# Sums for layer 2's logits placed in the other arms of layer 1's weight splits

## The chip, the cores and the metric

The kernel runs on one core of a Trainium2 chip. The metric is the time of the whole program on the device, in microseconds. A core has the engines TensorE (PE in the profile; its weight loads are PEld), VectorE (DVE), ScalarE (ACT), GpSimd (POOL) and SyncE (SP, which issues most of the DMAs). Each works through its own list of instructions in order, and they meet at semaphores.

## What is computed

An attention over pooled keys feeds two layers of a mixture of experts over 4608 tokens of 512 values, with 8 experts and 1024 hidden units. The change lies in the first of these layers, and in the gating of the second that is computed beside it.

```python
def _moe_ref(x, modality_id, w_gate, modality_bias, w1, w2):
    logits = x @ w_gate + modality_bias[modality_id]
    e_idx = np.argmax(logits, axis=1)
    ...                                   # gate_w: softmax of the logits, at e_idx
    for e in range(E):
        mask = e_idx == e
        h = np.maximum(x[mask] @ w1[e], 0.0)
        out[mask] = gate_w[mask, None] * (h @ w2[e])

def _moe2_ref(x, w_skip, w_gate, w1, w2):
    skip_score = x @ w_skip               # x: what layer 1 gives
    do_compute = skip_score > 0
    logits = x[do_compute] @ w_gate       # 8 logits a token
    ...                                   # as above; out = x + y where do_compute
```

So layer 2 needs nine dot products of 512 values for each token that layer 1 has finished: eight logits and the skip score. The kernel makes them on DVE.

## The kernel before

Layer 1 takes the tokens sorted by expert, in blocks of 256 (`T`). `Layer.body1(i, end)` writes out block `i`; what follows speaks of blocks 6 to 17. All engine work is in the order in which the code issues it; no scheduler moves it.

**The two products.** The first product is eight calls `m.gemm1(i, f)` (12 matmuls each, L1413): a hidden slice `f` of 128 for the 256 tokens. Numbers are split into a high and a low part, so three matmuls stand for one: `xh,w1h`, `xl,w1h`, `xh,w1l`. Behind every odd `f` ACT makes `hh` (the rectified high part) and DVE `hl` (the low part, L1418) for two slices at once. The second product is `m.gemm2(i, t, ...)` for each half `t` of the block's tokens (24 matmuls each, L1462: `w2h,hh`, `w2l,hh`, `w2h,hl` for `f` = 0 to 7). In the midst of `gemm2(i, 0)` PE transposes the next block's tokens (`next_x`, after `f` = 2 and 4), from which ACT makes `xh` and DVE `xl` (L1366). A block that is only half full skips `gemm2(i, 1)`. Block 13 of this input is one.

**A new expert.** Weights are split too. When block `i+1` has another expert than block `i` (the register `anew` tells it), the arms of four `If`s are taken: two of `split_w1_if` in block `i` (slices 0 to 3 ahead of `gemm2(i, 0)`, 4 to 7 behind it) and two of `split_w2_if` in block `i+1` (behind its `f` = 1 and `f` = 3). Each arm holds four casts on ACT (`w1h` or `w2h`) and four subtractions on DVE (`w1l`, L1333, or `w2l`, L1354). Among blocks 7 to 16 only 9 and 14 bring a new expert, and their arms run in full; the others skip them.

**The sums.** When half `t` of block `i` is done, `posts` puts nine sums on a list, `m.todo`: `logit`, one DVE instruction over 512 values (`hr`, L1743) with a short read of its accumulator (`lg`). So there are 18 a block. Behind the second half's nine stand the block's `picks`: `first` (ten small POOL operations, L1674 to L1684, and a maximum on DVE, `rt_mx`) and `second` (a maximum on DVE, `rt_my`, which waits for POOL's last `rt_eq`, then seven POOL operations, L1691 to L1696, that end in `M` and `rti`, then the block's store and scatter). `m.drip(n)` issues the next `n` entries. The calls of `drip` in `body1` are the order by hand: (1,1,1,2,1,2,1,1) behind the eight slices of the first product, one behind four or five of the slices in `gemm2(i, 0)`, and seven behind the second `split_w1_if`. The sums and picks of block `i` are thus worked off under block `i+1`.

**The ranks.** Behind `f` = 4 of the first product `rank` is called for the block before the last: two small matmuls on PE (`R`, L1722 and L1723) that read `M` and `rti`, then five short DVE operations (L1727 to L1731) and POOL work. PE stands until `rti` is there.

Of the kernel before, what the change touches and what calls it, by code (L numbers as in the profile page):

```python
# [1179 lines left out]
class Moe:  # L1180
# [154 lines left out]
    def load_split(self, i):  # L1335
        ET = mybir.EngineType
        self.anew = self.nc.values_load(self.g.r1.split[0:1, i:i + 1], min_val=0, max_val=1,
                                        engines=[ET.Activation, ET.DVE])

    def split_w1_if(self, fs):  # L1340

        with self.tc.If(self.anew > 0):  # L1342
            for f in fs:
                self.split_w1(f)
# [412 lines left out]
    def settle(self, i):  # L1757
        while any(x[0] <= i for x in self.todo):
            self.drip()

    def drip(self, n=1):
        while n > 0 and self.todo:
            _, cost, f = self.todo.pop(0)
            f()
            n -= cost


class Layer:
# [28 lines left out]
    def second(self):  # L1797

        m, g = self.m, self.m.g
        bg = g.bg  # L1800
        for f in range(8):
            m.gemm1(1, f)
            bg.tick()
            bg.tick()
        m.gemm2(1, 0, self.epilogue)
        bg.flush()
        self.gather(2)
        self.gather(3)
        self.load_regs(2)
        self.load_w1(2)  # L1810
        self.load_w2(2)
        m.load_split(2)
        m.split_w1_if(range(8))
        m.drip(7)
        m.gemm2(1, 1, self.epilogue, {3: lambda: m.xT(2, 0, m.ps_t("ps_x")),
                                      5: lambda: m.xT(2, 1, m.ps_t("ps_x")),
                                      6: lambda: m.gates1(2, m.sp)})
        m.gates2(2, m.sp)
        m.drip(5)
# [39 lines left out]
    def body(self, i):  # L1859
# [40 lines left out]
        with cmp.Else():  # L1900
            self.finish(i, full, turn, False)

    def body1(self, i, end):

        m = self.m
        late = i == self.n_static - 1
        ranks = m.ranks
        m.ranks = []
        for f in range(8):
            m.gemm1(i, f)  # L1910
            if f in (1, 3):
                m.split_w2_if(range(2 * f - 2, 2 * f + 2))
            m.drip(((0, 0, 1, 1, 1, 1, 2, 2) if late else (1, 1, 1, 2, 1, 2, 1, 1))[f])
            m.g.bg.tick()
            if f in (4, 6) and ranks:
                m.rank(ranks.pop(0))
            if f == 5 and i == self.n_static - 2:
                m.places2()
            if f == 6 and late:
                m.gather2(i + 1)  # L1920
                m.load_w1_parts(2, m.e2, end, range(4))
        m.rank_all(ranks)
        m.g.bg.flush()
        m.g.bg.pace = 2
        full = self.load_full(i)
        more = i + 1 < NBLK or end is not None
        if i + 1 < NBLK:
            self.load_w2(i + 1)
        if end is not None:
            m.load_w2_parts(2, m.e2, end)  # L1930

        def next_x(t):
            if t == 0 and end is not None:
                m.gates1(i + 1, m.sp)
            m.xT(i + 1, t, m.ps_t("ps_x"))
            if t == 1:
                m.gates2(i + 1, m.sp)

        if more:
            m.load_split(i + 1)  # L1940
            if end is None:
                m.gates1(i + 1, m.sp)
            m.split_w1_if(range(4))
        if end is None:
            at = {f: m.drip for f in ((0, 1, 5, 6) if i > 8 else (0, 1, 3, 5, 6))}
        elif late:
            at = {f: m.drip for f in (0, 1, 3, 5)}
        else:
            n = sum(x[1] for x in m.todo) - 2
            at = {f: partial(m.drip, (n + j) // 5) for j, f in enumerate((0, 1, 3, 5, 6))}  # L1950
            at[7] = m.drip
        if more and not late:
            at.update({2: lambda: next_x(0), 4: lambda: next_x(1)})
        m.gemm2(i, 0, self.epilogue, at)
        if late:
            _, _, second = m.todo.pop(0)
            m.drip(3)
            next_x(0)
            next_x(1)
            second()  # L1960
        if more:
            m.split_w1_if(range(4, 8))
        if end is None:
            m.drip(7)
        elif not late:
            m.drip()
        with m.tc.If(full > 0):
            m.gemm2(i, 1, self.epilogue)
# [126 lines left out]
```

## Time and profile before

| | us |
|---|---|
| runs (three) | 941.18, 945.1, 945.74 |
| median | 945.1 |
| profiled execution | 943.7 |
| its span, first to last instruction | 941.9 |
| PE busy | 893.1 (95% of the span) |
| DVE busy | 704.7 (75%) |
| POOL busy | 511.9 (54%) |
| ACT busy | 367.8 (39%) |
| mean granted TensorE clock | 0.981 |

In the profile a row names a line of the code, an engine, an operation, the tile written and the tiles read. In brackets stands how long the engine had been idle and what ended that. The clock is that of TensorE, granted by the throttle, as a share of full speed: 1.00 is 2.4 GHz, and its lower level, 1.2 GHz, would be 0.50. Block 7's first product starts at 367.87 us, block 9's at 415.05, block 10's at 444.33, block 13's at 515.09, block 14's at 533.67 and block 15's at 566.61.

### The profile page before, as it was taken

The numbers are of one execution on the slowest core, as the hardware profiler recorded it, in microseconds if no ns is written. First come the engines' busy times: TensorE is split into PE (matmuls) and PEld (weight loads), VectorE is DVE, ScalarE is ACT, GpSimd is POOL, SyncE is SP. The second block draws the span as 40 slices with busy tenths as digits, with TensorE's granted clock in tenths as the row PEclk, the third lists the DMA queues.
The fourth block names the chain that finished last, engine by engine and source line by source line (L and its number), as shares of the span: only waits on it lengthen the run. The fifth ranks groups of instructions, "written<-read, shape, count | busy, mean of one in ns | idle before, by whom it ended". The sixth has DMA issues, their size and how long they took to land. (4 is left out here: it accounts for less than half of the span.)

```text
span 941.9 us, 19066 instructions
## 1 busy us (share of the span) xinstructions
PE 893.1 (95%) x6231; PEld 803.2 (85%) x6231; DVE 704.7 (75%) x1816; ACT 367.8 (39%) x727; POOL 511.9 (54%) x762
## 2 busy tenths in 40 slices
PE   7899989899999999998999989999999999999995
PEld 6799889888899999987999869999888988979993
DVE  5467886787777888889877898777665777688663
ACT  3466656453222222251222422213413556565551
POOL 5766797303246647666766556575653443445442
PEclk9999999999999999999999999999989999999998
DMA  9999965513212211441224521227115673671341
GB/s 233 216 255 264 256 195 157 193 62 121 69 58 86 74 38 64 143 153 66 83 83 130 172 79 64 75 72 253 58 65 156 206 230 126 202 244 36 111 161 44
DMA packets 86141, 126.07 MB, mean 134 GB/s; under 512 B 13192, under 2 KB 50104, under 8 KB 85866
## 3 DMA queue, kind: packets, MB, share of 16 engines
q1 hardware_dynamic: 75386, 96.68, 33.4%
q0 software_dynamic: 10608, 27.67, 9.7%
q8 instruction: 63, 1.03, 0.5%
q14 instruction: 84, 0.69, 0.2%
HBM read 182.09 MB, written 39.50 MB: 235 GB/s over the span
## 5 line engine op out<-in xcount | busy, mean ns | idle before, releaser
L1413 PE MATMUL ps_g<-xh,w1h 128*128 128x256 f32 x896 | 256.4, 286 | 2.5 <-DVE o L1652 1.5
L1413 PE MATMUL ps_g<-xl,w1h 128*128 128x256 f32 x896 | 253.3, 283 | 2.2 <-DVE xl L1366 2.2
L1413 PE MATMUL ps_g<-xh,w1l 128*128 128x256 f32 x896 | 252.7, 282 | 0.0
L1743 DVE CUSTOM_DVE_ANT_0 hr<-x,W 128x512 bf16<-128x512 f32 x324 | 228.1, 704 | 19.1 <-DVEq L1342 6.3
L1462 PE MATMUL ps_g<-w2h,hh 128*128 128x512 f32 x464 | 190.6, 411 | 3.0 <-ACT w2h L1353 1.6
L1462 PE MATMUL ps_g<-w2h,hl 128*128 128x512 f32 x464 | 185.4, 400 | 6.2 <-DVE hl L1418 6.1
L1462 PE MATMUL ps_g<-w2l,hh 128*128 128x512 f32 x464 | 184.6, 398 | 0.0
L1413 PEld LDWEIGHTS ps_g<-xh,w1h 128*128 128x128 f32 x896 | 169.7, 189 | 7.2 <-issue 2.3
L1413 PEld LDWEIGHTS ps_g<-xl,w1h 128*128 128x128 f32 x896 | 169.2, 189 | 4.0 <-DVE xl L1366 3.0
L1413 PEld LDWEIGHTS ps_g<-xh,w1l 128*128 128x128 f32 x896 | 169.5, 189 | 0.0
L1417 ACT ACTIVATE hh<-ps_g 128x512 fp32r<-128x512 f32 (+1 forms) x116 | 67.7, 584 | 248.8 <-PE ps_g L1413 246.6
L1418 DVE SCALAR_TENSOR_TENSOR hl<-ps_g,hh 128x512 fp32r<-128x512 f32 (+1 forms) x116 | 77.5, 668 | 64.1 <-ACT hh L1417 40.0
L911 POOL TENSOR_SCALAR OB<-iota,BB,pay 128x128 bf16<-128x128 bf16 x126 | 111.7, 894 | 21.5 <-DVE BB L899 21.4
L1462 PEld LDWEIGHTS ps_g<-w2h,hl 128*128 128x128 f32 x464 | 88.2, 190 | 29.5 <-DVE hl L1418 7.7
L1462 PEld LDWEIGHTS ps_g<-w2h,hh 128*128 128x128 f32 x464 | 88.6, 191 | 21.4 <-issue 2.5
L1462 PEld LDWEIGHTS ps_g<-w2l,hh 128*128 128x128 f32 x464 | 88.5, 191 | 16.7
L1354 DVE TENSOR_TENSOR w2l<-w2r,w2h 128x512 fp32r<-128x512 f32 x112 | 75.3, 710 | 6.6 <-ACT w2h L1353 4.6
L1333 POOL TENSOR_TENSOR w1l<-w1r,w1h 128x512 fp32r<-128x512 f32 x35 | 45.3, 1314 | 59.7 <-ACT w1h L1330 59.4
L1709 POOL DMA_INDIRECT out_dram<-x,dsi x38 | 47.6, 1252 | 44.5 <-DMA out_dram<-x,dsi 16.8
L1353 ACT CAST w2h<-w2r 128x512 fp32r<-128x512 f32 x112 | 63.9, 617 | 0.0
L1330 ACT CAST w1h<-w1r 128x512 fp32r<-128x512 f32 x112 | 63.7, 620 | 0.5 <-ACT hh L1417 0.5
L1323 POOL DMA_INDIRECT xg<-xd,gidx x38 | 44.1, 1162 | 33.7 <-DVE rs_lo L1174 16.5
(298 smaller groups left out, 1399.9 us busy)
## 6 DMA issues: line engine op xcount, KB each, us to landing
w1r<-in_moe_w_dram SPq DMA_DIRECT2D x128, 512.0 KB
w2r<-in_moe_w_dram SPq DMA_DIRECT2D x124, 512.0 KB
x2s<-x SPq DMA_DIRECT2D x19, 522.0 KB
v<-in_v_dram SPq DMA_DIRECT2D x48, 192.0 KB
xd<-x SPq DMA_DIRECT2D x16, 520.0 KB
q_sb<-in_q_dram SPq DMA_DIRECT2D x16, 512.0 KB
kt<-in_k_dram SPq DMA_DIRECT2D x32, 144.0 KB
x2s<-OBx SPq DMA_DIRECT2D x16, 261.0 KB
```

What stands on the lines that cost most here:

```text
L911: e.tensor_scalar(g.ob(c)[:, i, :], g.iota, r.BB[:, c:c + 1], r.pay[:, i, c:c + 1], ALU.is_equal, ALU.mult)
L1323: self.nc.gpsimd.indirect_dma_start(out=self.xg[i % 2][:, t, 0:w], out_offset=None, in_=src, in_offset=bass.IndirectOffsetOnAxis(ap=gidx[: ...
L1330: self.nc.scalar.copy(self.w1h[f], raw)
L1333: low() if late is None else late.append(low)
L1353: self.nc.scalar.copy(self.w2h[f], raw)
L1354: (eng or self.nc.vector).tensor_tensor(self.w2l[f], raw, self.w2h[f].bitcast(F32), ALU.subtract)
L1413: nc.tensor.matmul(out, lhsT=a[f][:, k, :], rhs=b[:, k, :], start=(n == 0), stop=(n == 11))
L1417: nc.scalar.activation(out=hh, in_=whole, func=ACTF.Relu)
L1418: nc.vector.scalar_tensor_tensor(hl, in0=whole, scalar=0.0, in1=hh.bitcast(F32), op0=ALU.max, op1=ALU.subtract)
L1462: nc.tensor.matmul(ps, lhsT=a[f][:, tt], rhs=b[f], start=(n == 0), stop=(n == 23))
L1709: self.nc.gpsimd.indirect_dma_start(out=self.out, out_offset=bass.IndirectOffsetOnAxis(ap=self.dsi[i % 2][:, t:t + 1], axis=0), in_=self.x ...
L1743: self.nc.vector.tensor_tensor_reduce(out=self.junk, in0=self.x2[i % 2][:, t, 0:DM], in1=self.W9[:, e, :], scale=1.0, scalar=0.0, op0=ALU. ...
```

## The change

Four things move. (1) In blocks 6 to 15 (`arms`) the second split of `w1` becomes `sums_or_w1`: the new-expert arm holds the four splits, the other arm four of the block's own sums of half 0; the `rt_my` step (`second`) of the block before now stands behind this arm instead of ahead of it, and two more sums (`FREE`) follow. (2) In blocks 7 to 16 (`armed`) the two splits of `w2` become `sums_or_w2`: the other arms hold one sum and two sums. (3) Where a new expert took the arms, these seven sums are made up in `gemm2(i, 0)` behind `f` = 5 (`pick`, `sums_left`), ahead of `first`. (4) The calls of `drip` change: (0,0,1,0,1,0,1,1) in the first product, and 2, 1, 1 behind `f` = 0, 1, 3 of `gemm2(i, 0)`.

```diff
--- before.py
+++ after.py
@@ -1337,6 +1337,50 @@
         self.anew = self.nc.values_load(self.g.r1.split[0:1, i:i + 1], min_val=0, max_val=1,
                                         engines=[ET.Activation, ET.DVE])
 
+    COND, FREE = (4, 1, 2), 2
+
+    def load_split_dve(self, i):
+        return self.nc.values_load(self.g.r1.split[0:1, i:i + 1], min_val=0, max_val=1,
+                                   engines=[mybir.EngineType.DVE])
+
+    def sums_or_w1(self, i, fs):
+
+        while self.todo[1][0] < i:
+            self.drip()
+        (_, _, second), *todo = self.todo
+        sums = [x for x in todo if x[1]]
+        n = sum(self.COND)
+        self.cond = [f for _, _, f in sums[:n]]
+        with self.tc.If(self.anew > 0) as cmp:
+            for f in fs:
+                self.split_w1(f)
+        with cmp.Else():
+            for f in self.cond[:self.COND[0]]:
+                f()
+        second()
+        for _, cost, f in todo:
+            if not cost:
+                f()
+        self.todo = sums[n:]
+        self.drip(self.FREE)
+
+    def sums_or_w2(self, f):
+
+        c = self.COND
+        a = c[0] if f == 1 else c[0] + c[1]
+        with self.tc.If(self.anew > 0) as cmp:
+            for j in range(2 * f - 2, 2 * f + 2):
+                self.split_w2(j)
+        with cmp.Else():
+            for s in self.cond[a:a + c[1 if f == 1 else 2]]:
+                s()
+
+    def sums_left(self, new):
+
+        with self.tc.If(new > 0):
+            for s in self.cond:
+                s()
+
     def split_w1_if(self, fs):
 
         with self.tc.If(self.anew > 0):
@@ -1758,6 +1802,10 @@
         while any(x[0] <= i for x in self.todo):
             self.drip()
 
+    def settle_sums(self):
+        while len(self.todo) > 2:
+            self.drip()
+
     def drip(self, n=1):
         while n > 0 and self.todo:
             _, cost, f = self.todo.pop(0)
@@ -1900,17 +1948,25 @@
         with cmp.Else():
             self.finish(i, full, turn, False)
 
+    ARMS = 6
+
     def body1(self, i, end):
 
         m = self.m
         late = i == self.n_static - 1
+        arms = self.ARMS <= i < self.n_static - 2
+        armed = self.ARMS <= i - 1 < self.n_static - 2
         ranks = m.ranks
         m.ranks = []
         for f in range(8):
             m.gemm1(i, f)
             if f in (1, 3):
-                m.split_w2_if(range(2 * f - 2, 2 * f + 2))
-            m.drip(((0, 0, 1, 1, 1, 1, 2, 2) if late else (1, 1, 1, 2, 1, 2, 1, 1))[f])
+                if armed:
+                    m.sums_or_w2(f)
+                else:
+                    m.split_w2_if(range(2 * f - 2, 2 * f + 2))
+            m.drip(((0, 0, 1, 0, 1, 0, 1, 1) if armed else
+                    (0, 0, 1, 1, 1, 1, 2, 2) if late else (1, 1, 1, 2, 1, 2, 1, 1))[f])
             m.g.bg.tick()
             if f in (4, 6) and ranks:
                 m.rank(ranks.pop(0))
@@ -1936,12 +1992,22 @@
             if t == 1:
                 m.gates2(i + 1, m.sp)
 
+        if armed:
+            new = m.load_split_dve(i)
+
+            def pick():
+                m.settle_sums()
+                m.sums_left(new)
+                m.drip()
+
         if more:
             m.load_split(i + 1)
             if end is None:
                 m.gates1(i + 1, m.sp)
             m.split_w1_if(range(4))
-        if end is None:
+        if armed:
+            at = {0: partial(m.drip, 2), 1: m.drip, 3: m.drip, 5: pick}
+        elif end is None:
             at = {f: m.drip for f in ((0, 1, 5, 6) if i > 8 else (0, 1, 3, 5, 6))}
         elif late:
             at = {f: m.drip for f in (0, 1, 3, 5)}
@@ -1958,10 +2024,14 @@
             next_x(0)
             next_x(1)
             second()
-        if more:
+        if arms:
+            m.sums_or_w1(i, range(4, 8))
+        elif more:
             m.split_w1_if(range(4, 8))
-        if end is None:
-            m.drip(7)
+        if arms:
+            pass
+        elif end is None:
+            m.drip(8 if armed else 7)
         elif not late:
             m.drip()
         with m.tc.If(full > 0):
```

Two places show the order on DVE. The first is the end of block 9 and the start of block 10 (`rt_mx` and `rt_my` are the picks of block 8; `lg_3041` are the sums of block 9, `lg_3037` those of block 8; L1342 is the `If` of the split). Before:

```order
L1397 RECIPROCAL gate_2145<-g_su 128x2
L1681 TENSOR_REDUCE rt_mx<-lg_3037 128x2
L1690 TENSOR_REDUCE rt_my<-rt_eq 128x2
L1342 COMPARE_AND_BRANCH
L1333 TENSOR_TENSOR w1l_2565<-w1r_2148,w1h_2564 128x512 x2
...
L1342 UNCONDITIONAL_BRANCH x2
...
L1743 ISA hr,lg_3041<-x_3040,W_3044 128x512
...
L1418 SCALAR_TENSOR_TENSOR hl_2152<-ps_g_6384,hh_2151 128x512
```

With the change (L1380 is the `If` of `sums_left`, L1354 that of `sums_or_w1`; in the first of these arms stand seven sums, in the second's other arm four):

```order
L1441 RECIPROCAL gate_2145<-g_su 128x2
...
L1380 COMPARE_AND_BRANCH
L1787 ISA hr,lg_3037<-x_3036,W_3044 128x512
...
L1380 UNCONDITIONAL_BRANCH x2
L1725 TENSOR_REDUCE rt_mx<-lg_3037 128x2
L1354 COMPARE_AND_BRANCH
L1333 TENSOR_TENSOR w1l_2565<-w1r_2148,w1h_2564 128x512 x2
...
L1354 UNCONDITIONAL_BRANCH
L1787 ISA hr,lg_3041<-x_3040,W_3044 128x512
...
L1734 TENSOR_REDUCE rt_my<-rt_eq 128x2
...
L1462 SCALAR_TENSOR_TENSOR hl_2152<-ps_g_6437,hh_2151 128x512
```

The seven put-off sums have come ahead of `rt_mx`, four sums stand between `rt_mx` and `rt_my`, and between `rt_my` and the first `hl` of block 10 there are two sums where there were eight. The second place is DVE in block 13's second product, where `xl` of block 14 is made. Before:

```order
L1384 TENSOR_TENSOR gd_3051<-xg_2142,g_mx 128x2x8
L1342 COMPARE_AND_BRANCH
L1333 TENSOR_TENSOR w1l_2150<-w1r_2146,w1h_2149 128x512 x2
...
L1342 UNCONDITIONAL_BRANCH x2
L1743 ISA hr,lg_3037<-x_3036,W_3044 128x512
L1743 ISA lg_3037 128x1
L1681 TENSOR_REDUCE rt_mx<-lg_3037 128x2
L1366 TENSOR_TENSOR xl_2144<-ps_x,xh_2143 128x4x128 x2
```

With the change:

```order
L1428 TENSOR_TENSOR gd_3051<-xg_2142,g_mx 128x2x8
L1386 COMPARE_AND_BRANCH
L1333 TENSOR_TENSOR w1l_2150<-w1r_2146,w1h_2149 128x512 x2
...
L1386 UNCONDITIONAL_BRANCH x2
L1787 ISA hr,lg_3037<-x_3036,W_3044 128x512
...
L1410 TENSOR_TENSOR xl_2144<-ps_x,xh_2143 128x4x128
L1787 ISA hr,lg_3037<-x_3036,W_3044 128x512
L1787 ISA lg_3037 128x1
L1410 TENSOR_TENSOR xl_2144<-ps_x,xh_2143 128x4x128
```

Three sums stand ahead of the first `xl` and one between the two, where one sum and `rt_mx` stood ahead of both.

## Rows read from the trace of the kernel before

**Rows 1.** Waits of PE, 344 to 627 us: what for; us in total, times, longest.

```profile
PE ps_g L1462 <- DVE hl L1418: 6.1, 2, 3.5
PE ps_g L1413 <- DVE xl L1366: 1.5, 1, 1.5
PE R L1723 <- POOL rti L1696: 1.1, 1, 1.1
PE ps_g L1413 <- ACT xh L1363: 0.4, 1, 0.4
```

**Rows 2.** Windows: stretch, us, busy PE, PEld, DVE, ACT, POOL (count), PEclk, DMA, GB/s.

```profile
415.00:444.30 29.30, 25.61 (x155) 22.59 (x155) 25.29 (x69) 9.10 (x17) 18.81 (x38) 0.94 0.21 72
444.30:467.90 23.60, 23.60 (x155) 21.34 (x154) 20.58 (x61) 5.17 (x9) 18.71 (x31) 1.00 0.21 75
...
533.70:566.60 32.90, 27.70 (x154) 23.82 (x155) 29.50 (x80) 10.98 (x21) 19.49 (x41) 0.90 0.23 81
```

**Rows 3.** Windows, same columns, behind three waits of PE (clock before the DMA share).

```profile
425.00:430.00 5.00, 5.00 (x36) 4.55 (x35) 4.97 (x11) 1.20 (x2) 2.73 (x3) 1.00 0.16 46
...
435.00:440.00 5.00, 5.00 (x19) 4.12 (x19) 4.70 (x14) 1.65 (x4) 2.46 (x5) 0.71 0.00 0
...
537.00:540.50 3.50, 3.50 (x20) 3.50 (x18) 3.46 (x8) 0.61 (x2) 2.90 (x6) 0.53 0.19 70
```

**Rows 4.** Timeline of DVE, block 9's first product: start, us, instruction [idle before].

```profile
418.11 0.17 DVE L1690 TENSOR_REDUCE rt_my<-rt_eq 128x2 f32<-128x16 f32 x1 [1.78 <-POOL rt_eq L1684]
418.23 0.69 DVE L1743 CUSTOM_DVE_ANT_0 hr<-x,W 128x512 bf16<-128x512 f32 x1
...
423.25 0.69 DVE L1418 SCALAR_TENSOR_TENSOR hl<-ps_g,hh 128x512 fp32r<-128x512 f32 x1
423.86 2.48 DVE L1354 TENSOR_TENSOR w2l<-w2r,w2h 128x512 fp32r<-128x512 f32 x4
...
432.69 0.17 DVE L1727 TENSOR_TENSOR rt_rk<-M,R 128x16 f32<-128x16 bf16 x1
...
433.57 0.68 DVE L1418 SCALAR_TENSOR_TENSOR hl<-ps_g,hh 128x512 fp32r<-128x512 f32 x1
```

**Rows 5.** Timeline of PE, block 13: start of the first product, and `rank`'s matmul.

```profile
515.09 0.28 PE L1413 MATMUL ps_g<-xh,w1h 128*128 128x256 f32 x1
...
522.21 0.18 PE L1722 MATMUL R<-M,trim 128*128 128x16 bf16 x1
```

**Rows 6.** Timeline of DVE, block 13's second product, ahead of block 14.

```profile
530.07 0.22 DVE L1384 TENSOR_TENSOR gd<-xg,g_mx 128x16 f32<-128x16 f32 x1
531.12 2.50 DVE L1333 TENSOR_TENSOR w1l<-w1r,w1h 128x512 fp32r<-128x512 f32 x4 [0.83 <-ACT w1h L1330]
533.54 0.68 DVE L1743 CUSTOM_DVE_ANT_0 hr<-x,W 128x512 bf16<-128x512 f32 x1
...
534.23 1.28 DVE L1366 TENSOR_TENSOR xl<-ps_x,xh 128x512 fp32r<-128x512 f32 x2
```

**Rows 7.** Timelines of DVE (two rows) around the start of block 7's first product.

```profile
367.74 0.17 DVE L1681 TENSOR_REDUCE rt_mx<-lg 128x2 f32<-128x16 f32 x1
370.55 0.17 DVE L1690 TENSOR_REDUCE rt_my<-rt_eq 128x2 f32<-128x16 f32 x1 [2.64 <-POOL rt_eq L1684]
```

**Rows 8.** Timeline of POOL: first and last operations of three chains of `picks`.

```profile
367.89 0.20 POOL L1674 COPY x<-lg 128x18 f32<-128x18 f32 x1 [2.62 <-DVE lg L1743]
...
373.79 0.57 POOL L1696 CAST rti<-carry 128x8 bf16<-128x8 f32 x1
...
418.36 0.64 POOL L1691 TENSOR_TENSOR rt_eq<-rt_eq,rt_my 128x16 f32<-128x16 f32 x1 [0.28 <-DVE rt_my L1690]
...
422.71 0.66 POOL L1696 CAST rti<-carry 128x8 bf16<-128x8 f32 x1
...
638.78 0.22 POOL L1691 TENSOR_TENSOR rt_eq<-rt_eq,rt_my 128x16 f32<-128x16 f32 x1 [0.69 <-DVEq L1342]
...
640.84 0.19 POOL L1696 CAST rti<-carry 128x8 bf16<-128x8 f32 x1
```

## Prediction

> **What bounds the kernel now.** I read the windows by block first, then what PE waits for, then the engines at those waits. In layer 1 an ordinary block takes 23.60 us with PE busy for all of it; blocks 9 and 14, the two that bring a new expert, take 29.30 and 32.90 with PE busy for 25.61 and 27.70 [rows 2]. So the two cost 5.7 + 9.3 = 15.0 us more than ordinary blocks, and that is all that this change can win. Between 344 and 627 us PE has five waits [rows 1]: two for `hl`, 6.1 together (2.6 in block 9, 3.5 in block 14), 1.5 and 0.4 for `xl` and `xh` at the start of block 14, and 1.1 for `rti` at the ranks of block 9. That is 9.1. The other 5.9 is clock: behind the wait for `hl` the granted clock is 0.71 for 5 us, behind that for `xl` 0.53 for 3.5 us, while behind the wait of 1.1 it stays at 1.00 [rows 3]. Full speed is 2.4 GHz, 0.53 is nearly its lower level. Three waits lost clock, so **a wait of 1.9 us or more costs about 2.0 us on top**, and one of 1.1 nothing.
>
> Why `hl` is late: DVE works without a gap from `rt_my` at 418.11 to the `hl` at 433.57 for which PE stands [rows 4]. Seven sums lie between 418.23 and the first `hl` at 423.25, 0.72 each; four splits of `w2` take 2.48, 0.6 each [rows 4].
>
> **What goes.** From `rt_my` to that third `hl` there are 12 sums in block 9 now (7, 2 and 3 around the two splits), and 4 with the change (2, 1 and 1). In block 14 it is 13 against 4. That is 8 x 0.72 = 5.8 and 9 x 0.72 = 6.5 us less on DVE, against waits of 2.6 and 3.5: both go with 3 us to spare, and so does the clock behind them. Gain 6.1 + 2 x 2.0 = **10.1**. What was hidden behind `hl` is the last `hl`, which has two sums fewer as well; nothing else is late there. The wait of 1.1 for `rti` in block 9: `rt_my` stays where it is (four splits of `w1` lie ahead of it in both), but 2 sums run beside POOL's chain and then `w2l`, instead of 7 sums; I take 0.3 for it, **gain 0.8** (0 to 1.1).
>
> **What grows: the start of block 14.** Block 13 is half full, so no second half hides `xl`. DVE now passes from `gd` at 530.07 through a wait of 0.83 and four `w1l` to 533.54, then one sum and `rt_mx`, then both `xl` from 534.23 to 535.51 [rows 6], 1.5 us after PE wants them [rows 1], at 534.0. With the change three sums stand ahead of the first `xl` and one between the two. On the other side only one sum is left between the last two `hl`s of that block, where three were, so DVE comes to `gd` up to 1.0 earlier (ACT's casts behind it bound that). 533.54 - 1.0 + 3 x 0.72 + 0.6 + 0.72 + 0.6 = 536.6, a wait of 2.6 or, with the small operations, 2.8; 3.6 if DVE comes no earlier. The wait was 1.5 + 0.4 and has lost its clock already: **loss 0.9** (0.7 to 1.7).
>
> **What is new: the ranks of blocks 10 and 15.** The seven put-off sums must be done ahead of `rt_mx`, and behind that hangs a chain that PE needs: ten POOL operations, `rt_my`, seven POOL operations, `rti`, `R`. PE comes to `R` 522.21 - 515.09 = 7.1 us after the start of its first product [rows 5]. Take block 9. From `rt_my` at 418.11 on DVE has, up to the next `rt_mx`: 18 sums (13.0), 4 `hl` and 2 `xl` (0.6 each, 3.6), 8 `w2l` (4.8), the rank's five (0.9, from 432.69 to 433.57 [rows 4]) and some 1.5 of small operations and branches (`gd` is 0.22 [rows 6], `rt_mx` 0.17 [rows 7]): 23.8. It has no slack, so `rt_mx` comes at 441.9. Block 10 starts at 415.0 + 23.6 + 0.3 = 438.9: `rt_mx` stands 3.0 after it. The ten operations took 2.64 with DVE idle [rows 7]. With the change four sums run beside them, and POOL is slow beside sums: the seven operations took 638.78 to 641.03 alone, 2.2, and 418.36 to 423.37 beside sums and splits, 5.0, each 0.6 to 0.7 instead of 0.2 to 0.25 [rows 8]. So for the ten: 2.9 us beside four sums (some four operations), the other six alone in 1.6, `rt_my` at 3.0 + 4.5 + 0.2 = 7.7. At least it is 3.0 + 2.9 + 0.2 = 6.1, since the four sums stand ahead of it. The seven behind it run beside two sums, an `hl` and more sums: between 2.2 and 5.0, and I take the middle, 3.6. `rti` comes 11.3 after the start, bounds 8.3 and 12.7, so PE waits **4.2 at `R` (1.2 to 5.6)**, and the clock falls behind that: 6.2. Block 15 behind 14 has the same instructions. Two of them: **loss 12.4** (2.4, with no clock lost, to 15.2). On PE what is queued behind `R` are the slices 5 to 7 of the first product.
>
> That POOL is slow beside sums has a rule in the Trainium skill, "SBUF — State Buffer", section "Who interferes with whom": VectorE and GpSimd share a port pair, and who holds it locks the other out, when a VectorE instruction reads two operands from SBUF. It speaks against this change, which puts sums beside the ten operations, and the trace agrees (0.64 against 0.22 for the same subtraction [rows 8]). By the rule the two waits are there; without it the sum would be that of the first rival.
>
> **Ordinary blocks.** All 18 sums stay, and DVE has room (20.58 of 23.60 [rows 2]). `rt_my` moves behind four sums, to somewhere between 2 us ahead of the block's start and 0.5 behind it by the count of sums. Even with 5.0 for the seven operations `rti` is there at 5.5, ahead of 7.1: no cost. Block 7 is the exception: `rt_mx` is at -0.1 and `rt_my` at 2.7 there already [rows 7] (the block starts at 367.87), and the last `rti` at 374.36 [rows 8], 0.6 ahead of `R`. Block 6 is the first with arms, so four sums come beside the ten operations: about 2 us later, a wait of 1.2 (0 to 2.0, above 1.9 with clock). **Loss 1.2.** In blocks 14 and 16, where a full block with fewer small gaps precedes, I allow **0.5** (0 to 1.1). The extra register loads and branches lie on DVE, 0.2 to 0.5 us a block, in its slack.
>
> **The sum.** 943.7 (the profiled execution) - 10.1 - 0.8 + 0.9 + 12.4 + 1.2 + 0.5 = 943.7 + 4.1 = **947.8**. That execution lies 1.4 under the median of the runs.
>
> **Rivals.**
> - *POOL keeps pace.* If the sums beside the ten and the seven operations do not slow POOL, `rti` comes at 8.3, PE waits 1.2 and no clock falls; block 7 waits for nothing, and 0.5 and 0.3 go too: -10.1 - 1.1 + 0.9 + 2.4 = -7.9, 935.8. For it: in block 7 it took only 3.8 from the start of `rt_my`, 370.55 [rows 7], to the end of the last `rti`, 374.36 [rows 8], although DVE was making sums. Against it: 5.3 for the same in block 9 [rows 4, 8]. Chance 0.15.
> - *Half of it.* The ten are slowed, the seven run at 2.2: `rti` at 9.9, a wait of 2.8 plus 2.0. -10.1 - 0.8 + 0.9 + 9.6 + 0.6 = +0.2, 943.9. Chance 0.22.
> - *Slower: ordinary ranks are late as well.* `rt_my` 1.6 us later than I count is enough (0.5 + 1.6 + 5.0 = 7.1), since then PE waits at `R` in ordinary blocks too, six of them at 1.0 each: +4.1 + 6.0, 953.8; with block 7 losing clock 955.8. For it: DVE is the fuller engine and all its new work stands ahead of `rt_my`. Against: the slack of 3 us a block. Chance 0.13.
> - *The change doesn't remove the waits for `hl`.* If `hl` were late by ACT or by the weights' arrival, the 10.1 would stay lost: 957.9. Against it: DVE had no gap ahead of it [rows 4]. Chance 0.03.
>
> **How the numbers follow.** Forecast 947.8, chance 0.47, its own range 944.5 to 951.5 by the bounds of the rank's price. Within 0.5% of the median (4.7 us, about what a measurement can tell from no change) is between 940.4 and 949.8. Faster: the first rival and a tenth of the second, 0.17. Slower: a third of the forecast (0.15), and the last two rivals: 0.31. Same: 0.52. The range reaches down through most of the first rival and up to the lower part of the third: 935.5 to 953.5, which leaves out about 0.05 below and 0.12 above.
>
> **What would show it.** In the profile after: no wait for `hl` in blocks 9 and 14, and clock 1.00 there in the second product; waits of PE at `R` (its second matmul, behind `rti`) in blocks 10 and 15 of about 4 us, with the clock down behind them; the `xl` wait of block 14 at 2.8; ordinary blocks at 23.6; block 7 at about 24.8; POOL's ten operations at 4.5 where four sums run beside them. Wrong it would be if blocks 10 and 15 take 23.6 (then -10 or so), if a wait for `hl` stays, or if ordinary blocks grow.

## The result and the profile after

| | before | after |
|---|---|---|
| median of seven runs, us | 941.39 | 948.92 |
| lowest, highest | 938.85, 945.74 | 946.97, 952.13 |
| ratio after to before | | 1.0079, 95% interval 1.0058 to 1.0100 |
| profiled execution | 943.7 | 951.17 |
| its span | 941.9 | 949.5 |

The change makes the kernel 7.5 us slower. The time of a block, from the first matmul of its first product to that of the next block's, says where (us, both profiled executions):

| block | 7 | 8 | 9 | 10 | 11, 12 | 13 | 14 | 15 | 16 | 17 |
|---|---|---|---|---|---|---|---|---|---|---|
| before | 23.59 | 23.59 | 29.28 | 23.58 | 23.59 | 18.58 | 32.94 | 23.59 | 23.70 | 25.46 |
| after | 24.84 | 23.59 | 23.59 | 29.89 | 23.59 | 18.34 | 28.54 | 29.01 | 24.65 | 29.84 |
| difference | +1.25 | 0 | -5.69 | +6.31 | 0 | -0.24 | -4.40 | +5.42 | +0.95 | +4.38 |

These differences add up to +8.0. What lies ahead of block 7 took 1.55 less in this execution, and what lies behind block 17 took 1.1 more (0.6 of it a wait at `R` in block 19 that before does not have). Of these the change edits only the end of block 6, which took 23.73 in both.

What PE waits for in layer 1 after the change (the view of [rows 1]; 360 to 648 us, in total, times, longest):

```profile
PE R L1767 <- POOL rti L1740: 4.8, 4, 1.7
PE R L1766 <- POOL M L1737: 3.9, 2, 2.0
PE ps_g L1457 <- DVE xl L1410: 2.8, 1, 2.8
PE ps_x L1404 <- DMA xg<-x2s,gi: 2.4, 2, 1.7
PE R L923 <- DVE rc_cb L919: 0.8, 1, 0.8
```

Both waits for `hl` of [rows 1] are gone. In their place PE waits at `R` for `M` and `rti`, longer for `xl`, and for two things that were not in [rows 1] at all: `rc_cb`, and the gather of layer 2's tokens. The wait for `rc_cb` is in block 16, where PE begins layer 2's first count of tokens. DVE makes `rc_cb` from `carry`, and `carry` is written by the last POOL operations of the picks. Before, it was made without a wait 1.5 us after the block's start; now it comes at +3.6:

```profile
594.88 0.17 DVE L919 CAST rc_cb<-carry 128x8 bf16<-128x8 f32 x1 [1.25 <-POOL carry L1739]
```

The windows by block (columns as in [rows 2]; blocks 9, 10, 14, 15 and 17):

```profile
414.70:438.30 23.60, 23.60 (x155) 21.34 (x155) 21.65 (x56) 9.21 (x17) 14.25 (x24) 1.00 0.20 68
438.30:468.20 29.90, 26.22 (x155) 23.80 (x155) 23.48 (x70) 5.17 (x9) 19.16 (x35) 0.89 0.22 77
...
533.80:562.30 28.50, 25.42 (x155) 22.90 (x155) 26.31 (x70) 11.11 (x21) 15.57 (x27) 0.94 0.20 66
562.30:591.30 29.00, 25.37 (x155) 22.98 (x154) 23.30 (x70) 5.17 (x9) 18.48 (x34) 0.94 0.20 70
...
616.00:645.80 29.80, 27.43 (x215) 24.09 (x214) 21.85 (x69) 4.95 (x9) 22.65 (x38) 0.94 0.30 82
```

Block 9 now has the 23.60 of an ordinary block, and block 10 takes 29.90, where block 9 took 29.30. The excess has moved one block on, and with it the low clock. Windows behind three of the waits, in blocks 10, 14 and 17:

```profile
449.50:453.50 4.00, 4.00 (x20) 4.00 (x20) 3.36 (x13) 0.60 (x1) 1.25 (x1) 0.50 0.33 128
...
537.00:541.00 4.00, 4.00 (x22) 4.00 (x23) 3.41 (x8) 0.00 (x0) 2.72 (x8) 0.61 0.36 138
...
638.00:642.00 4.00, 3.83 (x13) 3.14 (x14) 2.15 (x9) 1.18 (x3) 3.12 (x12) 0.64 0.82 250
```

The chain that PE stands for in block 10 (which starts at 438.34). First DVE's timeline, the two steps of the picks:

```profile
441.24 0.17 DVE L1725 TENSOR_REDUCE rt_mx<-lg 128x2 f32<-128x16 f32 x1
...
445.64 0.17 DVE L1734 TENSOR_REDUCE rt_my<-rt_eq 128x2 f32<-128x16 f32 x1 [1.24 <-POOL rt_eq L1728]
```

Then POOL's, the ten operations and the seven that follow `rt_my`:

```profile
441.27 0.20 POOL L1718 COPY x<-lg 128x18 f32<-128x18 f32 x1 [8.09 <-DVE lg L1787]
441.42 0.18 POOL L1719 COPY x<-tokf 128x2 f32<-128x2 f32 x1
441.68 0.62 POOL L1720 TENSOR_SCALAR d_pos<-lg 128x2 f32<-128x2 f32 x1
...
443.80 0.70 POOL L1723 TENSOR_SCALAR d_val<-tokf 128x2 f32<-128x2 f32 x1
444.59 0.20 POOL L1724 TENSOR_TENSOR d_val<-d_val,d_pos 128x2 f32<-128x2 f32 x1
...
447.33 0.22 POOL L1737 TENSOR_TENSOR M<-M,d_val 128x16 bf16<-128x16 bf16 x1
...
449.23 0.19 POOL L1740 CAST rti<-carry 128x8 bf16<-128x8 f32 x1
```

And PE's, the two matmuls of `R`:

```profile
447.60 0.17 PE L1766 MATMUL R<-M,trim 128*128 128x16 bf16 x1 [1.98 <-POOL M L1737]
...
449.47 0.17 PE L1767 MATMUL R<-rti,ones 128*128 128x16 bf16 x1 [1.70 <-POOL rti L1740]
```

`rt_mx` stands 2.9 us behind the block's start. Four of the ten operations run beside the four sums and take 0.6 to 0.7 each; the sums are done at 444.4, and the others take 0.2. `rt_my` comes at +7.3, `rti` at +11.1, and PE, which came at +7.3, waits 3.7.

### The profile page after: what moved, and what is told of

Read it like the earlier page. It is cut to its first block, busy times and chain, and to the rows that moved or that the text cites. A ratio compares the mean times of both kernels' runs of the same rounds, so it can differ in the third digit from the quotient of the medians.

```text
span 949.5 us, 19105 instructions
## 1 busy us (share of the span) xinstructions
PE 895.5 (94%) x6231; PEld 806.4 (85%) x6231; DVE 704.1 (74%) x1816; ACT 368.7 (39%) x727; POOL 515.7 (54%) x762
## 5 line engine op out<-in xcount | busy, mean ns | idle before, releaser
L1457 PEld LDWEIGHTS ps_g<-xh,w1h 128*128 128x128 f32 x896 | 171.5, 191 | 11.7 <-issue 7.9
L1457 PEld LDWEIGHTS ps_g<-xl,w1h 128*128 128x128 f32 x896 | 171.2, 191 | 5.2 <-DVE xl L1410 4.3
L1457 PEld LDWEIGHTS ps_g<-xh,w1l 128*128 128x128 f32 x896 | 171.4, 191 | 0.0
L911 POOL TENSOR_SCALAR OB<-iota,BB,pay 128x128 bf16<-128x128 bf16 x126 | 116.2, 929 | 23.3 <-DVE BB L899 23.2
L1753 POOL DMA_INDIRECT out_dram<-x,dsi x38 | 44.8, 1179 | 49.6 <-DMA out_dram<-x,dsi 21.4
L1566 ACT ACTIVATE x<-ps_g,gate 128x512 f32<-128x512 f32 x37 | 25.5, 690 | 104.0 <-PE ps_g L1506 104.0
```

Of the source, the lines that this page charges most:

```text
L911: e.tensor_scalar(g.ob(c)[:, i, :], g.iota, r.BB[:, c:c + 1], r.pay[:, i, c:c + 1], ALU.is_equal, ALU.mult)
L1457: nc.tensor.matmul(out, lhsT=a[f][:, k, :], rhs=b[:, k, :], start=(n == 0), stop=(n == 11))
L1566: nc.scalar.activation(out=self.x2[i % 2][:, t, 0:DM], in_=ps, func=ACTF.Copy, scale=self.gate[i % 2][:, t:t + 1])
L1753: self.nc.gpsimd.indirect_dma_start(out=self.out, out_offset=bass.IndirectOffsetOnAxis(ap=self.dsi[i % 2][:, t:t + 1], axis=0), in_=self.x ...
```

## The experiments

All kernels are the changed one with one edit, except where a second is named. The ratios are to runs of the kernel before on the same chip.

| kernel | edit | median, us | ratio [95% interval] |
|---|---|---|---|
| `a_rank` | ranks behind the first product's last slice | 951.03 | 1.0075 [1.0050, 1.0100] |
| `b_end` | arms end one block earlier | 949.61 | 1.0069 [1.0046, 1.0091] |
| `c_xl` | sums behind `xl` | 958.78 | 1.0130 [1.0086, 1.0174] |
| `e_second` | `rt_my` ahead of the arm | 951.14 | 1.0069 [1.0041, 1.0096] |
| `leftout` | the put-off sums left out | 935.94 | 0.9945 [0.9922, 0.9967] |
| `lag12` | ranks one block later, up to block 11 | 944.15 | 1.0024 [1.0005, 1.0044] |
| `three` | three sums put off, not seven | 941.58 | 1.0001 [0.9979, 1.0023] |
| `spread` | five put off, sums later, ranks later | 946.15 | 1.0059 [1.0029, 1.0090] |
| `early` | arms in blocks 6 to 11 alone, ranks later | 935.72 | 0.9939 [0.9917, 0.9961] |

### Are the waits at `R` the price? (`a_rank`)

```diff
-            if f in (4, 6) and ranks:
+            if f in (4, 6) and ranks and not (armed and i < self.n_static - 2):
                 m.rank(ranks.pop(0))
```
What is left in `ranks` is ranked behind the loop over the slices.

> The changed kernel, but in blocks 7 to 15 the two matmuls `R` stand behind all eight slices of the first product instead of behind slice 4, so PE comes to them at 11.7 us after the block's start instead of 7.1. Theory (the waits at `R` are the price of the put-off sums, since `rti` is there 11.1 us after the start of blocks 10 and 15): no wait of PE at `R` in blocks 7, 10, 14, 15, and no fall of the clock behind it. Blocks 7, 10, 15 go from 24.84, 29.89, 29.01 back to 23.6, so the program gets about 13 us shorter than with the change, near 936. Rival 1 (the wait only moves, since the ranks' DVE operations now come late, ahead of the next `gd`): the waits for `R` go but a wait for `xl` or `hl` of 2 us or more takes their place in the same blocks, 944 to 949. Rival 2 (the waits at `R` cost nothing that a later wait would not take): 948.9.

The waits at `R` went, and the program got no shorter. PE's waits from 360 to 648 us:

```profile
PE ps_g L1457 <- DVE xl L1410: 4.0, 1, 4.0
PE R L923 <- DVE rc_cb L919: 4.0, 1, 4.0
PE ps_g L1457 <- DVE hl L1462: 3.8, 2, 2.5
PE ps_g L1457 <- ACT xh L1407: 1.1, 1, 1.1
PE ps_x L1404 <- DVE rt_rk L1771: 0.8, 1, 0.8
PE ps_x L1404 <- DMA xg<-x2s,gi: 0.5, 1, 0.5
```

They add up to 14.2, against 14.7 with the change. Block 10 took 27.85 instead of 29.89 and block 15 25.21 instead of 29.01, with waits for `hl` in the place of those for `R`; block 14 took 30.32 instead of 28.54 (`xl`, 4.0), and block 16 30.11 instead of 24.65 (layer 2's first count, `rc_cb`, 4.0). The theory, that `R` was the whole price, fell; the first rival came nearest, though block 15's wait for `hl` was 1.3 and not 2 or more. In block 16 the wait was again for `carry`, whose last write ended 6.7 us after the block's start (3.5 with the change). One of the new waits belongs to the edit itself: `ps_x <- rt_rk` is a transposed tile that waits for the PSUM buffer which the late rank still holds.

### Is the wait for the gather the change's doing? (`b_end`)

```diff
-        arms = self.ARMS <= i < self.n_static - 2
-        armed = self.ARMS <= i - 1 < self.n_static - 2
+        arms = self.ARMS <= i < self.n_static - 3
+        armed = self.ARMS <= i - 1 < self.n_static - 3
```

> The changed kernel, but the arms end one block earlier (blocks 6 to 14, and 7 to 15 for the splits of `w2`), so that block 16 has the order of before. Theory (block 17 grew from 25.46 to 29.84 because the picks made under block 16 come 2.8 us later and push the gathers of layer 2's first tokens back in POOL's queue): `rt_mx` is back at 5.4 us ahead of block 17, the wait of PE for `xg` in block 17 (2.4) is gone, block 17 takes 25.5, and the program is 4.4 us shorter than with the change, about 944.5. Rival (the gather's wait is a chance of the DMA queues in that run): block 17 still takes 27 to 30, 948 to 950.

`rt_mx` came back to 5.3 us ahead of block 17, and block 17 to 26.12; but block 16, without arms behind an armed block 15, took 25.85 instead of 24.65 (`rc_cb`, 2.0). The profiled execution gained 3.7 in blocks 7 to 17; in the medians the gain is not clear of noise, so the forecast of 25.5 and of 4.4 us less was met only in part. The wait of 0.4 that stayed has another reason: the picks, the scatters and the two other gathers stood as in before, but POOL's rank operation (`RH`) waited 1.7 for DVE, where the rank stood behind a step of layer 2's slots that waited 1.25 for PE. That the gather waits by the change and not by chance is shown better by all kernels together. POOL issues layer 2's first gather from `x2s` behind the picks, two scatters, two other gathers and a rank, and PE wants its rows some 19 us into block 17:

| kernel | `rt_mx` from block 17's start | first gather issued at | PE waits | block 17 |
|---|---|---|---|---|
| before | -5.39 | 15.30 | 0 | 25.46 |
| `early` | -5.34 | 15.30 | 0 | 25.46 |
| `b_end` | -5.31 | 16.46 | 0.4 | 26.12 |
| `a_rank` | -2.63 | 16.75 | 0.5 | 26.51 |
| `e_second` | -2.63 | 16.84 | 0.6 | 26.50 |
| `three` | -3.02 | 17.09 | 0.8 | 26.85 |
| `leftout` | -3.17 | 17.13 | 1.0 | 26.90 |
| after | -2.57 | 17.62 | 2.4 | 29.84 |
| `lag12` | -2.60 | 17.63 | 2.4 | 29.85 |
| `c_xl` | -1.83 | 17.99 | 2.7 | 29.94 |
| `spread` | +0.37 | 19.59 | 3.4 | 30.88 |

The wait follows the time of issue without exception, and from 2.4 on it costs about 2 us of clock as well. The issue follows the picks only roughly: in `e_second` the picks and the gathers ahead stood as in after, but POOL's rank operations took 0.8 less.

### Do the sums ahead of `xl` make block 14's wait? (`c_xl`)

```diff
-            at = {0: partial(m.drip, 2), 1: m.drip, 3: m.drip, 5: pick}
+            at = {5: pick}
```

> The changed kernel, but no sums stand in the second product ahead of `xl`: the four sums behind slices 0, 1 and 3 come with the fifth behind slice 5. Theory (block 14's wait for `xl`, 2.8 us and 1.9 of clock, is the three sums and the one ahead of it): the wait is 0 to 0.6, and block 14 takes 24 instead of 28.5, so 4.5 us less in that block; blocks 10 and 15 keep their waits for `R` of 3.7, since DVE is without a gap there; block 17 may grow by 0 to 2, since `rt_mx` comes later where DVE has gaps. Program 944.5 to 946.5. Rival (`xl` is late by ACT's casts, not by the sums): the wait stays at 2 or more, 948 to 949.

The wait for `xl` went to nothing, so the sums make it and not ACT. But block 14 took 30.98, more than with the change:

```profile
PE R L1766 <- POOL M L1737: 7.9, 3, 3.1
PE R L1767 <- POOL rti L1740: 6.9, 5, 1.9
PE ps_x L1404 <- DMA xg<-x2s,gi: 2.7, 2, 1.7
PE R L923 <- DVE rc_cb L919: 2.3, 1, 2.3
```

Waits at `R` now stand in block 14 too (3.1 and 1.9). The wait for `xl` had covered the lateness of the picks: `rti` was there 12.1 us after the block's start with the change and 12.7 here, but PE came to `R` at +11.9 with the change and at +7.6 here. Neither the forecast of 945 nor the rival held: the gain was given back in the same block, with interest. Blocks 9, 10, 15 and 16 grew by 0.8 to 1.5 each as well.

### POOL's pace or the order on DVE? (`e_second`)

```diff
     def sums_or_w1(self, i, fs):
         ...
+        second()
         with self.tc.If(self.anew > 0) as cmp:
         ...
-        second()
```

> The changed kernel, but `second` (with `rt_my`) stands ahead of the arm again, so the four sums run beside POOL's second chain of seven operations instead of beside its first of ten. Theory (POOL is slow beside sums, so it loses the time in one chain or the other): in blocks 10 and 15 the ten take 2.7 instead of 4.1, the seven stay at 4 to 5, `rti` is there 10 to 10.8 us after the start instead of 11.1, PE waits 2.8 to 3.5 at `R` with the clock falling as before, and the program is the same within 2 us, 947 to 949. Rival (the four sums delay `rt_my` only by standing ahead of it on DVE): `rti` is there at 8.1, the wait is 0.7 to 1.0, no clock falls, 937 to 940.

POOL's timeline in block 10 (which starts at 441.36):

```profile
445.49 0.20 POOL L1718 COPY x<-lg 128x18 f32<-128x18 f32 x1 [8.84 <-DVE lg L1787]
...
447.91 0.22 POOL L1728 TENSOR_TENSOR rt_eq<-rt_eq,desc 128x16 f32<-128x16 f32 x1
...
448.72 0.56 POOL L1736 TENSOR_SCALAR M<-rt_eq 128x16 bf16<-128x16 f32 x1
...
452.23 0.66 POOL L1740 CAST rti<-carry 128x8 bf16<-128x8 f32 x1
```

The ten took 2.6 (they took 4.3 with the change) and the seven 4.5 (3.5 with the change), from 448.42 to 452.89. So POOL loses its time beside sums in whichever chain they stand, and `rti` came at 11.5, not at the rival's 8.1. The size of the waits was missed: DVE, which now idles ahead of every `rt_my`, came to `rt_mx` itself 1.2 us later, and PE waited 1.9 at `R` and 1.8 a little before:

```profile
449.24 0.39 PE L1457 MATMUL ps_g<-xh,w1l 128*128 128x256 f32 x1 [1.80 <-DVE lg L1787]
```

This is the first matmul that reads `w1l` of slice 4, a weight that the arm writes when a new expert comes. With this edit the arm stands behind `rt_my` on DVE, and PE went on 0.05 us after the arm's first sum had ended (449.19). In block 15 the same matmul waited 1.1, and also went on 0.06 after that sum. So in block 10 the two waits add up to 3.7, as with the change. The rule in the Trainium skill, "SBUF — State Buffer", section "Who interferes with whom", fits these rows: a VectorE instruction that reads two operands from SBUF locks GpSimd's reads out (a sum reads `x` and `W`), one that reads at most one, outside the 2-port modes, does not. In the changed kernel the operation at 447.33 ran beside an `hl`, one of whose operands is in PSUM, and took 0.22.

### Is it the place of the put-off sums, or DVE's load? (`leftout`, `lag12`)

`leftout` issues the seven put-off sums nowhere. `lag12` issues all work, and makes the ranks of blocks 7 to 11 a block later.

```diff
 leftout:
                 m.settle_sums()
-                m.sums_left(new)
                 m.drip()
 lag12:
-        ranks = m.ranks
-        m.ranks = []
+        hold = self.ARMS < i < 12
+        n = len(m.ranks) - (1 if hold else 0)
+        ranks, m.ranks = m.ranks[:n], m.ranks[n:]
```

> The changed kernel without the seven put-off sums of the two new-expert blocks (14 sums are left out, so the logits of two blocks are incomplete). This takes 14 x 0.73 = 10.2 us off DVE at the one place. Theory now (what the change cannot win is DVE's own work: blocks 9 and 14 hold 23 us of it in 23.6, so each put-off sum is paid by a wait somewhere in the next blocks; with the sums gone nothing waits): `rt_mx` is there 2 us ahead of the start of blocks 10 and 15 instead of 2.9 behind it, no wait at `R` in 10 and 15, both take 23.6, block 9 stays at 23.6; the wait for `xl` in block 14 (2.8) and the one for the gather in block 17 stay. 11 to 12 us less than with the change, about 937 to 939. Rival (the price lies in the two register loads and branches and in the order of the picks): `R` still waits over 1.5 us in 10 and 15, 944 to 949.

Blocks 10 and 15 of `leftout`:

```profile
438.70:462.30 23.60, 23.60 (x155) 21.33 (x154) 18.33 (x57) 5.17 (x9) 17.29 (x32) 1.00 0.26 90
557.50:581.10 23.60, 23.60 (x156) 21.34 (x155) 17.91 (x53) 5.17 (x9) 15.24 (x29) 1.00 0.19 65
```

As expected: the put-off sums are the whole price in these two blocks. The register loads and the branches that stay cost PE nothing; the `If` of `sums_left` is left out here too, but with the change blocks 8, 11 and 12 run through all of them and took 23.59. The total, 935.9, lies 1 us under the forecast and says less, since layer 2 goes by incomplete logits here.

> The changed kernel, but in blocks 7 to 11 the ranks are made one block later than now (still behind slice 4), and block 12 makes two. PE's `R` then finds `rti` 12 us old, and the order on DVE, its load and the tiles of `xl` stay as they are. Theory now (the put-off work is paid wherever it is put): the waits at `R` in blocks 7 and 10 are gone, but in block 10 DVE is as late as before and the first `hl` comes at 9.4, so PE waits 1.5 to 2.5 for `hl` (a PSUM buffer of the first product comes free only then) and loses clock: block 10 takes 26.5 to 28 instead of 29.9; block 15, whose ranks are not moved, keeps its 29. 3 to 4.5 us less than with the change, 944 to 946. Rival (`R` was all of it): block 10 takes 23.6, 941 to 942.

Block 10 of `lag12`, and the only wait of PE in it, from PE's timeline:

```profile
437.40:461.60 24.20, 23.75 (x155) 21.33 (x154) 21.69 (x67) 5.07 (x9) 16.28 (x29) 1.00 0.21 73
```

```profile
446.67 0.38 PE L1457 MATMUL ps_g<-xh,w1h 128*128 128x256 f32 x1 [0.45 <-DVE hl L1462]
```

Here my theory of the moment, that the put-off work is paid wherever it is put, was too strong, and the rival was nearer, though the program's time lies in the theory's range: block 10 took 24.29, with 0.45 for `hl` and a clock of 1.00, although DVE was as late as before (`rt_mx` at +2.7). DVE was busy for 21.69 of the 24.20, so the block has room for the put-off sums, as long as nothing that PE needs soon hangs behind them. In `a_rank` the same block lost 4.3. The late ranks had pushed DVE's picks back from block 8 on: `rt_mx` of block 10 came at +4.6 there against +2.7 here, and the block's first `hl` at +10.5 against +8.6, 1.9 later in both. Block 10's own rank can't have made that wait, since its DVE operations came at +17.9. Block 15, where the ranks were not moved, kept 28.25, and the program lost two thirds of what the change had added.

### How much to put off (`three`, `spread`)

```diff
 three:
-    COND, FREE = (4, 1, 2), 2
+    COND, FREE = (0, 1, 2), 6
 spread, with the ranks as in lag12:
-    COND, FREE = (4, 1, 2), 2
+    COND, FREE = (1, 2, 2), 2
-            m.drip(((0, 0, 1, 0, 1, 0, 1, 1) if armed else
+            m.drip(((0, 0, 0, 0, 0, 2, 2, 2) if armed else
```

> The changed kernel with three sums of a block put off instead of seven: the arm at the split of `w1` holds no sums, and six instead of two follow `rt_my`. `rt_mx` then comes 4 x 0.73 = 2.9 us earlier in blocks 10 and 15, at the block's start, nothing stands between it and `rt_my`, and `rti` is there at 8 to 9: waits at `R` of 1.4 to 2.0 instead of 3.7. On the other side four more sums stand ahead of the third `hl` of blocks 9 and 14: 8 of 12, so `hl` waits about 1 us in block 9. Theory now (paid anywhere): block 9 takes 25 to 26, blocks 10 and 15 26 to 27.5, block 14 30 to 32; the program 946 to 949, within 3 us of the change. Rival (only work ahead of `rt_mx` costs): 9 at 23.6, 10 and 15 at 25, 14 as with the change, 939 to 941.

In `three` the other arm at `w1` is empty and is taken out. Block 9 took 24.93 (waits of 0.3 and 0.6), 10 and 15 took 25.11 and 25.17 (waits of 1.36 and 1.45 at `R`, no clock lost), 14 30.07, 16 27.19 and 17 26.85. So three sums put off make the kernel as fast as before and no faster. Blocks 9 and 14 were about as the theory said, but 10 and 15 took the 25 of the rival, and the program's 941.6 is nearer to the rival's 939 to 941 than to the theory's 946 to 949: the waits of 1.4 cost no clock, and block 17 waited only 0.8.

> The same idea with its late work spread so that no single wait of PE is over 1.2 us in blocks 9 and 10: five sums put off instead of seven (1 in the arm at `w1`, 2 and 2 in those at `w2`), the other sums of the first product behind slices 5 to 7 (two each, so that no sum but `FREE`'s two stands ahead of the third `hl`), and the ranks one block later in blocks 7 to 11 as in the run before this one. Theory now: waits of 0.5 to 1.1 us in blocks 9 and 10 with the clock at 1.00, so 9 takes 24 to 24.5 and 10 24.5 to 25, 5.5 us more than two ordinary blocks are never reached (before: 29.3 and 23.6). Block 14 keeps its wait for `xl`, somewhat longer (29.5 to 31), and block 15 its wait at `R` (27.5 to 29). Program 3 us under the kernel before and 9 to 11 under the change, 937 to 941. Rival (a wait of 1 us costs clock as well, or DVE's load shows as one long wait again): 9 and 10 together over 52, no faster than before.

Blocks 9 and 10 took 23.88 and 24.63, as expected. But the sums behind slices 6 and 7 pushed the work ahead of `xl` back (block 14: waits of 1.0 and 3.9, 30.58), and the picks ahead of block 17 (30.88). What was won early was lost at the end, 5 us more than I had expected.

### A version that beats both (`early`)

Blocks 9 and 10 together cost 52.86 before and 47.88 in `lag12`; from block 13 on the order of before was the best of all that had run with every sum in place. So the arms stand only where they pay:

```diff
-        arms = self.ARMS <= i < self.n_static - 2
-        armed = self.ARMS <= i - 1 < self.n_static - 2
+        arms = self.ARMS <= i < self.n_static - 6
+        armed = self.ARMS <= i - 1 < self.n_static - 6
```

with the ranks of blocks 7 to 10 one block later, as in `lag12`.

> The changed kernel with the arms only in blocks 6 to 11 (those at `w2` in 7 to 12) and the ranks of blocks 7 to 10 one block later; from block 13 on the order is that of before. Theory now (a put-off sum is cheap where ordinary blocks with room on DVE follow and nothing on PE waits for the picks, and dear where layer 2's gathers are near): block 9 takes 23.6, block 10 24.3 (a wait for `hl` of 0.5), together 47.9 against 52.9 before; block 13 0.5 to 1 more than before, 14 33 to 33.5, 15 to 17 as before (23.6, 23.7, 25.5). Sum -4 to -5: 937 to 938.5, and 10 to 11 us less than with the change. Rival (the end of the arms costs in blocks 12 to 14 what blocks 9 and 10 gain): 941 to 943, no different from before.

PE's waits from 360 to 648 us, then the windows of blocks 10 and 9:

```profile
PE ps_g L1506 <- DVE hl L1462: 3.5, 1, 3.5
PE ps_g L1457 <- DVE xl L1410: 1.6, 1, 1.6
PE ps_g L1457 <- DVE hl L1462: 1.0, 2, 0.6
PE ps_g L1457 <- ACT xh L1407: 0.2, 1, 0.2
```

```profile
436.60:460.80 24.20, 23.76 (x155) 21.34 (x154) 21.70 (x67) 5.07 (x9) 16.30 (x29) 1.00 0.21 73
413.00:436.60 23.60, 23.60 (x156) 21.34 (x155) 21.65 (x56) 9.20 (x17) 14.04 (x23) 1.00 0.20 68
```

Blocks 9 and 10 take 23.59 and 24.29, block 14 33.26, 15 to 17 what they took before. The ratio to before is 0.9939 [0.9917, 0.9961], 6.6 us by the medians: 4.8 from blocks 7 to 17 in the profiled executions, as forecast. The rest is open, and part of it may be chance: block 19, which no edit touches, took 33.85 before at a clock of 0.90 and 32.00 here at 1.00, behind waits of about 2 us in both. `early` is fitted to where this input's new experts fall; with one at another block its gain would be another.

## Why the prediction was right, and where it was not

The measured 948.9 lies 1.1 from the forecast 947.8, but that is partly luck. With four more runs the median of before fell from 945.1 to 941.4, so the change is +7.5 and not +4.1, and the outcome is the one that had 0.31, slower by over 0.5%, not the likeliest.

**The gain** (10.1 for two waits for `hl` and their clock, 0.8 for `rti` in block 9): right. Block 9 gave 5.69, all that it had.

**The ranks of blocks 10 and 15** (12.4): right, nearly to the step. `rt_mx` at +3.0 was 2.9, `rt_my` at +7.7 was 7.3, `rti` at +11.3 was 11.1, the wait of 4.2 was 3.7, and the two blocks lost 6.31 and 5.42 together 11.7. The pace of POOL beside sums, which carried this term, was read from another place [rows 8] and held here.

**Block 14's `xl`**: a wait of 2.8 forecast, 2.81 measured. **Block 7**: 1.2 forecast, +1.25 measured. The small term of 0.5 for late ranks was 0.3 in block 14; block 16 lost 0.95, not at its rank but at layer 2's count.

**The step that failed** is "Ordinary blocks": that with `rti` ahead of `R` the later picks cost nothing. I followed the chain from the picks to `R` and stopped. Behind them hang `carry` and with it layer 2's count in block 16, and on POOL the scatters and, in block 17, the gathers of layer 2's first tokens, for which PE has transposes waiting. These were in the kernel's text and in before's trace, but [rows 1] ends ahead of the transposes, and before has no wait at them that could point there. POOL's first gather and PE's transposes in block 17 before (it starts at 613.90):

```profile
629.20 1.11 POOL L1323 DMA_INDIRECT xg<-x2s,gi  x1 [0.16 <-issue]
```

```profile
632.92 1.03 PE L1360 MATMUL ps_x<-ident,xg 128*128 128x128 f32 x8
```

And after the change (it starts at 615.96):

```profile
633.58 1.11 POOL L1323 DMA_INDIRECT xg<-x2s,gi  x1 [0.16 <-issue]
```

```profile
635.82 0.66 PE L1404 MATMUL ps_x<-ident,xg 128*128 128x128 f32 x4 [0.68 <-DMA xg<-x2s,gi]
...
638.17 0.66 PE L1404 MATMUL ps_x<-ident,xg 128*128 128x128 f32 x4 [1.69 <-DMA xg<-x2s,gi]
```

That is +4.38 in block 17, of which the sum had nothing; with it the +4.1 becomes 8.5, against 8.0 in blocks 7 to 17. The rival for the slower side had the right cause, picks that come too late, but looked for it at `R` in ordinary blocks: 8, 11 and 12 did not grow at all, and 16 grew at another matmul.

**The other rivals.** POOL did not keep pace: the ten operations took 4.3 and the seven 3.5. "Half of it" needed the seven at 2.2, and did not come either. That the waits for `hl` would stay was wrong.

## What to carry to other kernels

Work that is put off under a condition comes back at the place where it is made up; ask there, as for any moved step, what hangs behind it on every engine, down to the last queue, and not only to the first wait. Here the same seven sums cost 6 us where a rank that PE needs 7 us into the block hung behind them, and 0.7 where it was used a block later; picks moved back by 3 to 4 us cost nothing in blocks 11 to 13, by 4.2 us they cost 0.95 in block 16, where a count read what they write, and by 2.8 us they cost 4.4 in block 17, where a gather stood behind them. Taking one wait away shows only who is next: two of the kernels that removed a wait gave back all that it had held, or more.

## What the runs showed that I had not expected

A wait's price in clock is not read from its length alone, and the prediction's price, about 2.0 for 1.9 us or more, does not hold everywhere. Waits of 1.1 to 1.45 us cost none (block 7 after, blocks 10 and 15 of `three`). One of 1.8 in block 16 of `three` cost 1.7, while waits of 2.0 and 2.3 at the same matmul in `b_end` and `c_xl` cost 0.2; the two waits of block 10 after, 3.7 together, cost 2.6 and those of block 15, 3.6 together, 1.8 (block time less wait less the time of the same block without one). What tells them apart stayed open.
